# Top-32 attention with a squared-ReLU MLP: blocks of queries handled in pairs, PSUM banks fixed by purpose, MLP chunks of 512 rows

## Chip, cores and metric

One core of a Trainium2 chip. The metric is the device time of one execution in microseconds (us); lower is better.

## What is computed

```python
# q, k, v: (8, 8, 576, 64) float32; w_in: (512, 2048); w_out: (2048, 512)
scores = np.matmul(q, k.transpose(0, 1, 3, 2)) / np.sqrt(64)
kth    = np.partition(scores, -32, axis=-1)[..., -32:-31]      # the 32nd largest of a row
scores = np.where(scores >= kth, scores, -1e9)
attn   = softmax(scores)                                       # along a row
x      = matmul(attn, v) -> (8 * 576, 512)                     # heads side by side
out    = np.maximum(x @ w_in, 0) ** 2 @ w_out                  # (4608, 512) float32
```

## The kernel before

The program is written as a plan. Each operation is given an engine, an estimated duration, a priority (a due time), the tiles that it reads, writes and takes, and `schedule` turns the plan into one fixed order for each engine: when an engine is free, it takes the ready operation with the lowest priority. `Emitter` writes these orders out with semaphore waits. On the chip each engine then runs its own list in order and stands still at a wait.

**Blocks.** A row of scores has 576 columns. One block is 128 query rows of one head; the last 64 queries of both heads of a pair form one more block. 8 batches x 4 head pairs x 9 blocks are 288 blocks. `top_k` is called for a group of queries of a head pair and does its two blocks (three for the last group) with separate instructions for each block.

For one block (`top_k`, lines 443 to 573):

1. PE multiplies q and k in fp32 into two PSUM banks, 288 columns in each (`scores`, L365). One fp32 matmul appears in the trace as two passes; the two heads lie in different halves of the array's rows.
2. ACT copies the 576 scores to SBUF tile `s` (L464).
3. DVE takes the maximum of the two halves, one operand from PSUM: `m`, 288 wide (L528), then the maximum of the halves of `m`: `pp`, 144 wide (L535).
4. POOL makes the smaller values without comparing: it adds the two inputs as integers (L520, tiles `t1`, `t2`) and subtracts the maximum. The candidates lie in `f`: quarter maxima 0 to 144, their partners 144 to 288, the rest 288 to 576.
5. DVE finds eight values and strikes them out, three times (MAX8 and MATCH_REPLACE8): over 144, 144 and 288 columns. A last MAX8 over 576 columns (L561) gives the 32nd value, `kth`.
6. ACT makes `w` = relu(kth - s) in bf16, which is above zero where a score is to be dropped (L569).

`attend` then computes the scores once more, transposed (k times q, fp32, 64 rows of the array per head), adds `w` times a matrix with a very negative diagonal (`steep_bf`, the masks), and ACT takes the exponential out of PSUM (L628, L641). PE multiplies by v (`vb`, a column of ones gives the sum), DVE takes the reciprocal (L669), POOL scales (L671), PE transposes back. `feed` is the MLP over a chunk of rows: 576 rows of a batch in two halves of 288, the last batch as 320, 128 and 128.

The eight PSUM banks are one pool (`psum`); a tile of two banks or one bank goes wherever room is free. At the end `verdict` compares each kth with the eighth values struck out before. If one of the rounds had struck out too much, the whole program would be run again with full-width searches.

The constants `PER` (planned us per block), `T0` and `ME` (how much earlier than its block's other DVE work `m` is due) set the due times.

Of the kernel before, what the change touches and what calls it, by code (L numbers as in the profile page):

```python
# [12 lines left out]
P = 128  # L13
# [71 lines left out]
class Plan:  # L85
# [32 lines left out]
    def schedule(self, t0=0.0, latency=0.12, own=0.07):  # L118
# [162 lines left out]
def bass_top_k_attn__then__act_relu_squared_kernel(  # L281
# [11 lines left out]
    NHP = 4  # L293
# [8 lines left out]
    def sb(name, shape, dt=FP32, n=None):  # L302
# [3 lines left out]

    ident32 = sb("ident32", [P, P])
# [4 lines left out]
    kth = sb("kth", [P, 3, 4 * NPAIR + 8])  # L312
    c16 = sb("c16", [P, 3, 4 * NPAIR + 8])
    c24 = sb("c24", [P, 3, 4 * NPAIR + 8])
# [7 lines left out]

    sizes = {
        "rq": ([P, 5, 2, D], FP32, 2), "rk": ([P, 5, 2, D], FP32, 2), "rv": ([P, 9, D], FP32, 2),
        "qk": ([P, 2, S], FP32, 5), "vb": ([P, 10, D + 1], BF16, 5),
        "s": ([P, S], FP32, 8), "m": ([P, HALF], FP32, 4), "pp": ([P, QUART], FP32, 4),
        "t1": ([P, HALF], FP32, 2), "t2": ([P, QUART], FP32, 2), "f": ([P, S], FP32, 4),
        "a": ([P, 3, 8], FP32, 3), "sh": ([P, 3], FP32, 2), "w": ([P, S], BF16, 13),
        "p": ([P, 4, 2, 320], BF16, 3), "p4": ([P, 320], BF16, 3), "av": ([P, 5, D + 1], FP32, 2),
        "x": ([P, 5, D], BF16, 2), "xt": ([P, NCT, S], BF16, 3), "g": ([P, S], BF16, 16),  # L330
        "o": ([P, DM], FP32, 2), "ws": ([P, 1024], FP32, 2),
    }
    mem = {nm: sb(nm, *spec) for nm, spec in sizes.items()}
    pools = {nm: Pool(nm, spec[2]) for nm, spec in sizes.items()}
    ps32 = nc.alloc_psum_tensor("ps", [P, 8, 512], FP32)
    ps16 = ps32[:, :, :].bitcast(BF16)
    psum = Pool("psum", 8)
# [7 lines left out]
    def bank(t, i=0):  # L345
        return ps32[:, t.slot + i, :]
# [5 lines left out]

    def batch_order(b):
        if b < NB - 1:
            return ([(hp, g) for hp in range(NHP) for g in range(4)], {1: ([0, 1], False), 3: ([2, 3], True)},
                    [(0, S)])
        return ([(hp, g) for g in (2, 3, 0, 1) for hp in range(NHP)],
                {3: ([2, 3], True), 0: ([0], False), 1: ([1], False)}, [(256, 320), (0, 128), (128, 128)])

    PER = 3.2  # L360
    ME = 10
    T0 = 12.0
# [4 lines left out]
    def tr(o, i, ident):  # L367
# [557 lines left out]
```

## Time and profile before

| | |
|---|---|
| median of 3 runs | 1004.65 us (1004.55 to 1009.77) |
| profiled execution, its own time | 1005.76 us |
| span of its trace | 1003.8 us |
| mean granted TensorE clock | 0.968 |
| busy: PE, DVE, ACT, POOL | 910.8, 927.3, 765.0, 836.6 us |
| share of the span | 91%, 92%, 76%, 83% |

Busy time is the union of an engine's instructions. Instructions overlap at their ends (the next one starts while the last one drains), so the step from one start to the next is shorter than the mean duration of one; matmuls overlap most, and a busy PE is not PE at its peak.

### The profile page before, as it was taken

The numbers are of one execution on the slowest core, as the hardware profiler recorded it, in microseconds if no ns is written. First come the engines' busy times: TensorE is split into PE (matmuls) and PEld (weight loads), VectorE is DVE, ScalarE is ACT, GpSimd is POOL, SyncE is SP. The second block draws the span as 40 slices with busy tenths as digits, with TensorE's granted clock in tenths as the row PEclk, the third lists the DMA queues.
The fourth block names the chain that finished last, engine by engine and source line by source line (L and its number), as shares of the span: only waits on it lengthen the run. The fifth ranks groups of instructions, "written<-read, shape, count | busy, mean of one in ns | idle before, by whom it ended". The sixth has DMA issues, their size and how long they took to land.

```text
span 1003.8 us, 23634 instructions
## 1 busy us (share of the span) xinstructions
PE 910.8 (91%) x8082; PEld 537.9 (54%) x8082; DVE 927.3 (92%) x3538; ACT 765.0 (76%) x1341; POOL 836.6 (83%) x1391
## 2 busy tenths in 40 slices
PE   5677778999999999899999999899998999899996
PEld 3444444655555556555556555565565554456554
DVE  5999999999999999999999899999999999999920
ACT  4566668986799778897799868897788876668752
POOL 7998999888878888788888888797887878899941
PEclk9888799999999999999999999999999999899999
DMA  6643312011131102011211113101220110000001
GB/s 138 181 120 108 92 31 62 14 47 34 40 71 26 35 29 57 15 47 49 55 44 24 46 36 76 36 13 34 58 58 18 39 46 17 2 1 13 33 17 41
DMA packets 124417, 47.75 MB, mean 48 GB/s; under 512 B 116608, under 2 KB 116608, under 8 KB 124288
## 3 DMA queue, kind: packets, MB, share of 16 engines
q1 hardware_dynamic: 124288, 46.16, 18.1%
q8 instruction: 65, 1.06, 0.5%
q14 instruction: 64, 0.52, 0.2%
HBM read 36.70 MB, written 9.44 MB: 46 GB/s over the span
## 4 chain that ended last, share of the span: by engine, by line
POOL 36%; DVE 26%; PE 19%; issue 12%; ACT 5%; SPq 1%; DMA 1%; POOLq 0%; DVEq 0%
POOL f L520 18%; PE ps L365 18%; POOL t L520 13%; DVE kth L561 6%; DVE f L558 5%; DVE c L555 4%; DVE m L528 4%; DVE pp L535 3%; POOL x L671 2%; DVE f L549 2%; DVE a L547 2%; POOL vb L427 1%; ACT w L569 1%; ACT s L464 1%; ACT p L628 1%
## 5 line engine op out<-in xcount | busy, mean ns | idle before, releaser
L365 PE MATMUL ps<-qk 64*128 64x288 f32 (+7 forms) x2640 | 430.1, 438 | 45.3 <-DVE m L528 32.0
L365 PEld LDWEIGHTS ps<-qk 64*128 64x128 f32 (+1 forms) x2640 | 212.9, 181 | 169.8 <-DVE m L528 57.7
L569 ACT ACTIVATE w<-s,kth 128x576 bf16<-128x576 f32 x288 | 216.1, 776 | 28.4 <-DVE kth L561 27.4
L520 POOL TENSOR_TENSOR t<-s 128x288 int32<-128x288 int32 x288 | 229.2, 797 | 9.9 <-ACT s L464 7.5
L520 POOL TENSOR_TENSOR f<-t,m 128x288 int32<-128x288 int32 x288 | 223.9, 795 | 0.0
L464 ACT COPY s<-ps 128x576 f32<-128x576 f32 x288 | 170.8, 642 | 62.9 <-PE ps L365 62.3
L520 POOL TENSOR_TENSOR f<-t,pp 128x144 int32<-128x144 int32 x288 | 135.7, 489 | 99.4 <-DVE pp L535 99.2
L628 ACT ACTIVATE p<-ps 128x640 bf16<-128x640 f32 (+1 forms) x192 | 155.5, 812 | 74.2 <-PE ps L365 73.3
L558 DVE MATCH_REPLACE8 f<-c,f 128x144 f32<-128x144 f32 (+1 forms) x576 | 207.8, 368 | 0.0
L561 DVE MAX8 kth<-f 128x8 f32<-128x576 f32 x288 | 202.8, 747 | 0.0
L555 DVE MAX8 c<-f 128x8 f32<-128x144 f32 (+1 forms) x576 | 192.6, 372 | 2.1 <-POOL f L520 2.0
L365 PE MATMUL ps<-wo,g 128*128 128x512 bf16 (+1 forms) x640 | 158.8, 381 | 0.6 <-ACT xt L688 0.5
L365 PE MATMUL ps<-xt,win 128*128 128x288 bf16 (+2 forms) x1088 | 145.2, 283 | 5.4 <-DVE m L528 3.3
L528 DVE TENSOR_TENSOR m<-ps,s 128x288 f32<-128x288 f32 x288 | 126.8, 447 | 22.0 <-ACT s L464 18.2
L520 POOL TENSOR_TENSOR t<-m 128x144 int32<-128x144 int32 x288 | 141.4, 492 | 2.3
L365 PEld LDWEIGHTS ps<-steep_bf,w 128*128 128x128 bf16 (+1 forms) x1600 | 81.9, 101 | 108.5 <-issue 107.6
L365 PE MATMUL ps<-steep_bf,w 128*128 128x128 bf16 (+3 forms) x1600 | 121.9, 220 | 0.0
L535 DVE TENSOR_REDUCE pp<-m 128x144 f32<-128x288 f32 x288 | 116.1, 445 | 0.1
L365 PEld LDWEIGHTS ps<-xt,win 128*128 128x128 bf16 x1088 | 94.7, 99 | 37.6 <-DVE m L528 5.9
L365 PEld LDWEIGHTS ps<-wo,g 128*128 128x128 bf16 (+1 forms) x640 | 55.6, 100 | 57.3 <-issue 6.4
L549 DVE MATCH_REPLACE8 f<-a,pp 128x144 f32<-128x144 f32 x288 | 82.0, 293 | 0.0
L712 ACT ACTIVATE g<-ps 128x576 bf16<-128x576 f32 x112 | 71.9, 654 | 7.9 <-PE ps L365 6.8
(54 smaller groups left out, 780.8 us busy)
## 6 DMA issues: line engine op xcount, KB each, us to landing
rq<-in_q_dram SPq DMA_DIRECT2D x64, 128.0 KB, 2.4
rk<-in_k_dram SPq DMA_DIRECT2D x64, 128.0 KB, 2.5
rv<-in_v_dram SPq DMA_DIRECT2D x64, 128.0 KB, 2.4
out_dram<-o SPq DMA_DIRECT2D x32, 256.0 KB, 2.1
ws<-in_moe_w_in_dram SPq DMA_DIRECT2D x8, 512.0 KB, 5.2
ws<-in_moe_w_out_dram SPq DMA_DIRECT2D x8, 512.0 KB, 4.2
rq<-in_q_dram SPq DMA_DIRECT2D x32, 32.0 KB, 2.5
rk<-in_k_dram SPq DMA_DIRECT2D x32, 32.0 KB, 2.5
```

The lines of the kernel that those rows point to most:

```text
L365: return pe.matmul(o, l, r, start=start, stop=stop, skip_group_check=True)
L464: cp.append(pl.op("act", .64, tg - 28 + i, lambda i=i: act.copy(at(st[i])[:, :].rearrange("p (a c) -> p a c", a=2), ps32[:, ss[i].slot:ss[ ...
L520: return pl.op("gp", dur, prio + .8 * i, lambda: gp.tensor_tensor(o().bitcast(I32), x().bitcast(I32), y().bitcast(I32), op), **kw)
L528: dve(.43, lambda i=i: vec.tensor_tensor(at(m[i])[:, :], bank(ss[i])[:, 0:HALF], at(st[i])[:, HALF:S], ALU.max), dp=-ME, r=[ss[i]], hold=[ ...
L535: dve(.375, lambda i=i: vec.tensor_reduce(at(pp[i])[:, :], at(m[i])[:, :].rearrange("p (a c) -> p c a", a=2), AX.X, ALU.max), r=[m[i]], w= ...
L549: prev[i] = [dve(.275, lambda i=i: vec.match_replace(at(f[i])[:, 0:QUART], at(a)[:, i, :], at(pp[i])[:, :], NEG), r=[pp[i]], hold=[a], w=[ ...
L555: lambda i=i, t=t, wd=wd: vec.max(eighth(t, i), at(f[i])[:, 0:wd]),
L558: prev[i] = [chain(t, i, prev[i], dur + .06, lambda i=i, t=t, wd=wd: vec.match_replace(at(f[i])[:, 0:wd], eighth(t, i), at(f[i])[:, 0:wd], ...
L561: ks.append(chain(kth, i, prev[i] + [low[i]], .665, lambda i=i: vec.max(eighth(kth, i), at(f[i])[:, :]), hold=[f[i]]))
L569: pl.op("act", .75, tw + .8 * i, lambda i=i: act.activation(at(ws[i])[:, :], at(st[i])[:, :], ACTF.Relu, bias=kth[:, i, ix[i]:ix[i] + 1], ...
L628: return act.activation(o, i, ACTF.Exp, scale=0.125)
L712: return act.activation(at(g)[:, 0:nt].rearrange("p (a c) -> p a c", a=2), ps32[:, hh.slot:hh.slot + 2, 0:hw], ACTF.Relu)
```

## The change

- Two blocks are one unit. Their scores lie side by side in 1152 contiguous PSUM columns (three banks): five matmul pieces instead of four of 288 columns, the last one behind a wait on PE itself. One ACT copy of 1152, one `m` of 2x288, one reduction of 2x144 (written straight into `f`), and four POOL operations for the pair.
- The last 64 queries of two neighbouring head pairs form a unit of their own (`Z`). There are 144 units; `PER` becomes 6.0 for one unit.
- The three searches cover columns 0 to 104, 20 to 144 and 0 to 272 (before 0 to 144, 0 to 144, 0 to 288). The eighth value of the first is checked too (`c8`).
- `attend` no longer multiplies k by q: PE transposes `s` with the fp32 identity (nine 128x128 transposes for a pair), adds nine masks, and one ACT exponential reads 1152 columns.
- PSUM: banks 0 to 2 for scores, 3 to 5 for the transposed scores, one tile each; banks 6 and 7 for everything else.
- The MLP takes chunks of 512 rows; the 64-row remainders of six batches form one chunk of 384 rows, those of the last two lie in another.
- Weights are staged in the memory of `g`. The first loads of q, k and v wait for POOL to clear parts of `rv`.

```diff
-                        lat = own if v.eng == x.eng else latency
+                        lat = (own if x.eng != "pe" else .25) if v.eng == x.eng else latency
-    psum = Pool("psum", 8)
+    ps_s, ps_e, psum = Pool("ps_s", 1), Pool("ps_e", 1), Pool("psum", 2)
+    BASE = {"ps_s": 0, "ps_e": 3, "psum": 6}
...
+            PIECES = [[(0, 0, 0, 512, True), (1, 576, 512, 64, True), (1, 640, 0, 384, False), (1, 1024, 384, 128, True)],
+                      [(0, 512, 512, 64, False)]]
+            o_s = pl.op("pe", 1.2, tg - LEAD, lambda: fs(0), r=qu, w=[ss], take=[ss, st])
+            pl.op("pe", .15, tg - LEAD, lambda: fs(1), r=qu, w=[ss], after=[o_s])
+            cp = pl.op("act", 1.15, tg - LEAD + 1, lambda: act.copy(
+                at(st)[:, :, :].rearrange("p i c -> p (i c)"), wide(ss)), r=[ss], w=[st])
...
+                dve(.7, lambda: vec.tensor_tensor(
+                    at(m)[:, :, :], wide(ss).rearrange("p (i c) -> p i c", i=2)[:, :, 0:HALF],
+                    at(st)[:, :, HALF:S], ALU.max), dp=-ME, r=[ss], hold=[st], after=[cp], w=[m], take=[m])
+                big = dve(.67, lambda: vec.tensor_reduce(
+                    at(f)[:, :, 0:QUART], at(m)[:, :, :].rearrange("p i (a c) -> p i c a", a=2), AX.X, ALU.max),
+                    dp=-MQ, r=[m], w=[f], take=[f])
+                mid = whole(.87, tg - MP, ALU.subtract, lambda: at(f)[:, :, QUART:HALF], lambda: at(t2)[:, :, :],
+                            lambda: at(f)[:, :, 0:QUART], r=[t2], hold=[f], after=[big])
...
-                for t, wd, dur, more in ((c16, QUART, .215, None), (c24, HALF, .365, mid)):
+                for t, c0, c1 in ((c8, 0, 104), (c16, 20, QUART), (c24, 0, 272)):
...
+                        prev[i] = [chain(t, i, prev[i] + [mid], dur + .06,
+                                         lambda i=i, t=t, c0=c0, c1=c1: vec.match_replace(
+                                             at(f)[:, i, c0:c1], eighth(t, i), at(f)[:, i, c0:c1], NEG), hold=[f])]
...
+                for o, c, start in outs:
+                    tr(o, sf[:, c:c + 128], ident32[:, :], start=start, stop=True)
+                for o, c, start in outs:
+                    ins = mm(o, wf[:, c:c + 128], minus[:, :], False)
...
+            pl.op("act", 1.15, tt + 1, lambda: act.activation(
+                at(pt)[:, :, :].rearrange("p k q -> p (k q)"), wide(e), ACTF.Exp, scale=0.125), r=[e], w=[pt])
...
+        if o.eng == "sp":
+            o.deps.update(zeros)
```

DVE in the middle of the program; here are the rows of one unit before (`m` of later blocks stands between the searches; `pp`, `a`, `c` and `kth` are the steps above).

```order
L555 MAX c<-f 128x8 x2
L558 MATCH_REPLACE f<-c,f 128x144 x2
L555 MAX c<-f 128x8
L528 TENSOR_TENSOR m<-ps,s 128x288
L555 MAX c<-f 128x8
L528 TENSOR_TENSOR m<-ps,s 128x288
L669 RECIPROCAL rzall<-av 128x4
L558 MATCH_REPLACE f<-c,f 128x288 x2
L561 MAX kth<-f 128x8 x2
L535 TENSOR_REDUCE pp<-m 128x144 x2
```

DVE after, at the same place, with buffer numbers and waits (`s_gp` is POOL, `s_act` ACT, `s_dve` DVE itself): the start of unit f1, with the reduction of the next unit and an `m` between its own steps.

```order
1227 L563 TENSOR_REDUCE f1<-m1 128x2x144
1228 L563 TENSOR_REDUCE f2<-m2 128x2x144
1229 L578 MAX c8<-f1 128x8 [waits s_dve]
1230 L578 MAX c8<-f1 128x8
1231 L558 TENSOR_TENSOR m0<-ps,s3 128x576 [waits s_act]
1232 L582 MATCH_REPLACE f1<-c8,f1 128x104 [waits s_gp,s_dve]
1233 L582 MATCH_REPLACE f1<-c8,f1 128x104 [waits s_dve]
1234 L578 MAX c16<-f1 128x8 [waits s_dve] x2
```

Behind it: `m` and the reduction are one row for a pair, and the first MATCH_REPLACE of a unit waits for POOL, where before the third search did.

PE in the middle of the program after the change: scores of one unit (`qk`), transposes (`ident,s`) and masks (`steep_bf,w`) of another, and the transposes of a loaded k.

```order
L408 MATMUL ps<-qk 128x512 [waits s_dve]
L408 MATMUL ps<-qk 128x64
L408 MATMUL ps<-qk 128x384
L408 MATMUL ps<-qk 128x128
L411 MATMUL ps<-ident,s 128x128 [waits s_act]
L411 MATMUL ps<-ident,s 128x128 x3
L408 MATMUL ps<-steep_bf,w 128x128 x4
L408 MATMUL ps<-qk 128x64 [waits s_pe]
L411 MATMUL ps<-ident,rk 128x128 [waits d_rk0,s_act]
```

Behind it: every unit's scores wait for DVE's `m` of the unit before, which reads the same three banks.

The DMA queue at the start of the program after the change (before, the loads of q came first and without a wait).

```order
L826 DMA g<-in_moe_w_in_dram 128x1024 x2
L427 DMA rq<-in_q_dram 128x4x64 [waits s_gp]
L427 DMA rq<-in_q_dram 128x4x64
L429 DMA rq<-in_q_dram 64x2x64
L427 DMA rk<-in_k_dram 128x4x64 x2
```

Two transfers of weights now go ahead of the first loads.

## Rows read from the trace of the kernel before

**Rows 1.** The page: busy us, share of the span, instructions.

```profile
PE 910.8 (91%) x8082; PEld 537.9 (54%) x8082; DVE 927.3 (92%) x3538; ACT 765.0 (76%) x1341; POOL 836.6 (83%) x1391
```

**Rows 2.** Stretches: length, busy us of PE, PEld, DVE, ACT, POOL; clock, DMA.

```profile
50.00:150.00 100.00, 77.00 (x682) 46.54 (x681) 93.68 (x363) 65.88 (x113) 92.11 (x148) 0.83 0.32 87
...
400.00:600.00 200.00, 190.93 (x1707) 110.91 (x1706) 195.92 (x753) 164.82 (x289) 167.58 (x281) 0.99 0.16 41
...
940.00:970.00 30.00, 29.61 (x285) 18.72 (x285) 18.49 (x65) 19.00 (x41) 22.25 (x36) 1.00 0.07 24
```

**Rows 3.** DVE in order of time: start, length, line, operation, count.

```profile
503.17 1.18 DVE L535 TENSOR_REDUCE pp<-m 128x144 f32<-128x288 f32 x3
504.27 0.72 DVE L547 MAX8 a<-pp 128x8 f32<-128x144 f32 x3
...
507.55 0.82 DVE L555 MAX8 c<-f 128x8 f32<-128x288 f32 x2
...
510.64 2.07 DVE L561 MAX8 kth<-f 128x8 f32<-128x576 f32 x3
```

**Rows 4.** Groups by shape, DVE and POOL: count, busy us, mean ns, idle before.

```profile
L528 DVE TENSOR_TENSOR m<-ps,s 128x288 f32<-128x288 f32 x288 | 126.8, 447 | 22.0 <-ACT s L464 18.2 <-POOL f L520 2.1
L561 DVE MAX8 kth<-f 128x8 f32<-128x576 f32 x288 | 202.8, 747 | 0.0
...
L555 DVE MAX8 c<-f 128x8 f32<-128x288 f32 x288 | 119.3, 448 | 2.0 <-POOL f L520 2.0
...
L520 POOL TENSOR_TENSOR t<-s 128x288 int32<-128x288 int32 x288 | 229.2, 797 | 9.9 <-ACT s L464 7.5
...
L520 POOL TENSOR_TENSOR f<-t,pp 128x144 int32<-128x144 int32 x288 | 135.7, 489 | 99.4 <-DVE pp L535 99.2
```

**Rows 5.** PE in order of time, 500 to 513 us, and a run at 938 us.

```profile
501.67 1.13 PE L365 MATMUL ps<-qk 64*128 64x256 f32 x8
502.74 0.62 PE L365 MATMUL ps<-steep_bf,w 128*128 128x128 bf16 x8
503.31 1.24 PE L365 MATMUL ps<-qk 64*128 64x288 f32 x8
...
504.97 0.66 PE L368 MATMUL ps<-ident,rq 128*128 128x128 f32 x4
...
938.17 1.89 PE L365 MATMUL ps<-wo,g 128*128 128x512 bf16 x8
```

**Rows 6.** PE groups on the page: count, busy us, mean ns.

```profile
L365 PE MATMUL ps<-qk 64*128 64x288 f32 (+7 forms) x2640 | 430.1, 438 | 45.3 <-DVE m L528 32.0
...
L365 PE MATMUL ps<-wo,g 128*128 128x512 bf16 (+1 forms) x640 | 158.8, 381 | 0.6 <-ACT xt L688 0.5
L365 PE MATMUL ps<-xt,win 128*128 128x288 bf16 (+2 forms) x1088 | 145.2, 283 | 5.4 <-DVE m L528 3.3
...
L365 PE MATMUL ps<-steep_bf,w 128*128 128x128 bf16 (+3 forms) x1600 | 121.9, 220 | 0.0
```

**Rows 7.** ACT groups by shape: count, busy us, mean ns.

```profile
L464 ACT COPY s<-ps 128x576 f32<-128x576 f32 x288 | 170.8, 642 | 62.9 <-PE ps L365 62.3
...
L628 ACT ACTIVATE p<-ps 128x640 bf16<-128x640 f32 x128 | 90.0, 707 | 35.5 <-PE ps L365 34.9
...
L628 ACT ACTIVATE p<-ps 128x1024 bf16<-128x1024 f32 x64 | 65.4, 1022 | 38.7 <-PE ps L365 38.4
```

**Rows 8.** The first microseconds in order of time, and the weight loads on the page.

```profile
11.21 0.46 DVE L528 TENSOR_TENSOR m<-ps,s 128x288 f32<-128x288 f32 x1 [11.21 <-ACT s L464]
...
ws<-in_moe_w_in_dram SPq DMA_DIRECT2D x8, 512.0 KB, 5.2
```

**Rows 9.** The end: the last kth, ACT's last copy; a PE group from 940 to 970.

```profile
954.10 1.41 DVE L561 MAX8 kth<-f 128x8 f32<-128x576 f32 x2
...
996.08 0.59 ACT L745 COPY o<-ps 128x512 f32<-128x512 f32 x1 [3.08 <-PE ps L365]
...
L365 PE MATMUL ps<-xt,win 128*128 128x320 bf16 x64 | 10.1, 300 | 0.0
```

More of the change, by code (lines that the diff above doesn't have):

```diff
@@ L305, in sb @@
         return [nc.alloc_sbuf_tensor(f"{name}{i}", shape, dt) for i in range(n)]
+    PER = 6.0
+    T0 = 12.0
+    LEAD = 20
+    ME = 10
+    MQ = 0
+    MP = 3
+    LAG = 20
+    STEP = 3.2
     ident32 = sb("ident32", [P, P])
@@ L560, in top_k @@
-                for i in range(nb):
-                    ks.append(chain(kth, i, prev[i] + [low[i]], .665, lambda i=i: vec.max(
-                        eighth(kth, i), at(f[i])[:, :]), hold=[f[i]]))
+                dve(.7, lambda: vec.tensor_tensor(
+                    at(m)[:, :, :], wide(ss).rearrange("p (i c) -> p i c", i=2)[:, :, 0:HALF],
+                    at(st)[:, :, HALF:S], ALU.max), dp=-ME, r=[ss], hold=[st], after=[cp], w=[m], take=[m])
+                whole(1.45, tg, ALU.add, lambda: at(t1)[:, :, :], lambda: at(st)[:, :, 0:HALF],
+                      lambda: at(st)[:, :, HALF:S], r=[st], w=[t1], take=[t1])
@@ L578, in top_k @@
+                return st, wt
+            for i in range(2):
+                o = pl.op("gp", .75, tw + 1.3 * i, lambda i=i: gp.tensor_scalar(
+                    at(f)[:, i, :], at(st)[:, i, :], kth[:, i, n:n + 1], STEEP, ALU.subtract, ALU.mult),
+                    r=[st], hold=[f], after=[ks[i]])
                 pl.op("gp", .75, tw + 1.3 * i + .65, lambda i=i: gp.tensor_scalar(
-                    at(ws[i])[:, :], at(st[i])[:, :], BIG, at(sh)[:, i:i + 1], ALU.min, ALU.max),
-                    r=[st[i], sh], w=[ws[i]], take=[ws[i]])
@@ L685, in fx, with out_x @@
                 return ins
             pl.op("pe", .05 * nu + .1, tt + 5, fx, r=[xr], w=[xp], take=[xp])
-            pl.op("act", .19 + nq / 1200, tt + 6, lambda: act.copy(
-                at(xt)[:, hp, col:col + nq], ps16[:, xp.slot, 0:nq]), r=[xp], w=[xt], take=[xt] if first_xt else [])
-        def feed(b, tok, nt, xt, tm, step, end):
-            last = b == NB - 1
+            xt, col, first = parts
+            def out_x():
+                nq = 64 * nu
+                if gi != Z:
+                    return act.copy(at(xt)[:, hp, col:col + nq], half(xp)[:, 0:nq])
+                return act.copy(at(xt)[:, hp:hp + 2, col:col + 64],
+                                half(xp)[:, 0:128].rearrange("p (i q) -> p i q", i=2))
@@ L694, in feed @@
+            pl.op("act", .19 + nu / 20, tt + 6, out_x, r=[xp], w=[xt], take=[xt] if first else [])
+        def feed(chunk, xt, tm, step):
+            nt = sum(n_ for _, _, n_ in chunk)
+            b = chunk[-1][0]
+            last, end = b == NB - 1, chunk is CHUNKS[-1]
             kf = max(1, 512 // nt)
-            nh = 2 if nt > 512 else 1
-            hw = nt // nh
+            lag = 0 if last else LAG
             gs = [tile("g") for _ in range(NFB // kf)]
             for i, g in enumerate(gs):
-                hh = Tile(psum, nh)
+                hh = Tile(psum)
@@ L771, in build @@
[L771 to L777 removed]
+                hps = (hp, hp if gi != Z else hp + 1)
```

475 lines of the change are left out of this document (213 added, 262 removed).

## Prediction

> **What bounds the kernel now.** I read the page first, then stretches of the span, then each engine's list in order of time. On the page DVE (927.3 us) and PE (910.8) are both above 90% [rows 1], so their shares alone do not tell which sets the pace. The stretches do. From 400 to 600 us DVE is busy 195.92 of 200 us, while PE shows 190.93, ACT 164.82 and POOL 167.58 [rows 2]; PE's figure contains the draining ends of its matmuls. DVE's own idle time is small: all 288 `m` together wait 22.0 us, and the 288-wide searches wait 2.0 us for POOL [rows 4]. So DVE, with its fixed list, is the bound in the body. At the end it is PE: the last kth is ready at 955.5 (954.10 + 1.41), yet the last output copy starts at 996.08 [rows 9], and from 940 to 970 PE is busy 29.61 of 30 us [rows 2].
>
> The span of 1003.8 thus divides into 11.2 us before DVE's first instruction [rows 8], 944.3 us to the last kth, and 48.3 us behind it. The profiled execution took 1005.76 us; the median of the runs is 1.1 us below that.
>
> **DVE, the main term.** I take steps from start to start, since neighbours overlap. Two MAX8 of 288 take 0.82 where one lasts 0.448: a step of 0.37. Three of 144 take 0.72 and three of 576 take 2.07, which gives steps of about 0.21 and 0.66 [rows 3, 4]. A step is thus about 0.06 us plus 1.04 ns for each column. For `m` and the reduction I take 0.365 for 288 inputs (three reductions take 1.18 [rows 3]), hence 0.665 for one of 576.
> - Pairing `m` and the reduction saves a fixed part each: 2 x (0.73 - 0.665) = 0.13 us per pair.
> - The searches lose 40, 20 and 16 columns; each is a MAX8 and a MATCH_REPLACE8 in two blocks: 76 x 4 x 1.04 ns = 0.32 us per pair. The 576-wide last search stays.
> - 0.45 us x 144 pairs = **64 us less**. Some 17 reciprocals more cost about 1.5 us.
>
> DVE's list then lasts about 865 us, 5.9 us per pair.
>
> Whether a removed instruction gives back its whole duration or only its fixed step is decided here. By the rows an instruction starts 0.08 us before the one ahead of it ends [rows 3, 4], so only the step counts. The Trainium skill, "VectorE: DVE Perf Modes", section "The DRAIN you can't avoid", says that the next operation does not start until the pipeline is empty. The trace does not agree: the overlap is in the rows, so I keep the step. What whole durations would give is among the rivals.
>
> **A new wait on that path.** The first MATCH_REPLACE8 of a pair now waits for POOL's subtraction, because it overwrites what POOL reads. That subtraction can start only behind the reduction and lasts about 0.8 us (a 288-element operation takes 797 ns [rows 4]). Between the reduction and the waiting instruction the order puts two short MAX8 (0.34 us) and mostly an `m` or the next reduction (0.66 each), so 1.0 to 1.7 us. With semaphores the work fits in most places. Nothing to all is between 0 and about 0.5 us x 144 = 72 us; since the cover is there in the order, I take +5 us for this and for waits at `m` together.
>
> **POOL and ACT.** A POOL element costs (797 - 489) / 144 = 2.1 ns, so an operation on 576 takes about 1.41 us and a pair costs 2 x (1.41 + 0.80) = 4.4 instead of 5.2 us: some 105 us less in all, with squares for a few more chunks (+15) on top. ACT's one copy of 1152 and one exponential of 1152 cost about 1.1 us each by the slope between 640 and 1024 columns ((1022 - 707) / 384 = 0.82 ns [rows 7]), slightly less than now. Neither sets the pace, so I count nothing; the fifth DMA of each v load is on a queue with room.
>
> **PE, the resource that gets tighter.** Steady steps: eight fp32 passes of 288 take 1.24 us with the last one's 0.44 in it; eight masks 0.62; four fp32 transposes 0.66; eight matmuls of 512 take 1.89 with 0.38 in it, 0.215 each or 0.42 ns per bf16 column [rows 5, 6].
> - Scores: today the two heads alternate, and one pass of each head streams beside one of the other, so four matmuls cost about 1.0 us per pair. Now one head has one 512-column matmul, the other three in a row, and the remaining 64 columns come alone. Counting what cannot lie side by side, 512 + 512 + 384 + 128 + 128 + 128 columns at the 0.84 ns of today's passes: about 1.5 us. **+0.5 us per pair.**
> - Transposed scores: 2.0 us per pair now (for four blocks 2 x (1.07 + 0.57) from the starts in [rows 5], and 0.8, four passes and four masks, for the last 64 keys); nine transposes at about 0.13 and nine masks at about 0.07: 1.8 us. **-0.2 us.**
> - MLP: the first product keeps its columns, the second has 36 row blocks instead of 40, since the half-filled ones of 64 rows go: 64 matmuls x 0.215, about **-15 us in all**.
>
> By steps, PE's work is now about 2640 x 0.12 + 640 x 0.215 + 1088 x 0.12 + 1600 x 0.058 [rows 6] plus some 95 us for v, loads and transposes: 775 us. It becomes about 775 + 43 - 15 = 800 us. In a span of 945 that is 85%, against 77% now. It fits, but waits cost more.
>
> **Start.** Two 512 KB weight loads (5.2 us to landing [rows 8]) now go ahead of q, and q waits for POOL's clearing. That is 2 to 5 us; the first unit needs 1.5 times the score work and a copy twice as long, 1 to 2 us more. DVE starts at 14 to 18 us. I take **+5**.
>
> **End.** Behind the last kth of the new order PE has about 61 matmuls of 512, 112 of 128 columns and one unit's transposes and products: 13 + 6.5 + 2.5 = 22 us, plus two relus of 576 before (1.3, as copies of that width [rows 7]) and what follows ACT's last copy today (7.7). That is 32 to 37 us against 48.3, if PE is on schedule; being tighter, it may bring a backlog along. Between 0 and -15 I take **-8**.
>
> **Sum.** 1005.8 - 64 + 1.5 + 5 + 5 - 8 = 945 us, so far from 1004.65 that the 1.1 us do not matter.
>
> **The rivals.**
> - *Everything fits better* (start hidden, PE on time, end -15): 1005.8 - 64 + 1.5 + 3 - 15 = about 930 down to 918. For it: POOL and ACT both get freer. Against: two single PSUM buffers and a third of two banks, each a ring. 0.10.
> - *Whole durations count.* Then pairing gives 2 x (2 x 0.447 - 0.747) = 0.29 us per pair instead of 0.13, so 88 instead of 64 us: 921. Against: by this count DVE's 288-wide groups alone could not fit their busy time (288 x 0.448 = 129 us against 119.3 [rows 4]). It is the rule of the section named above. 0.03.
> - *PE becomes the bound.* From 940 to 970 PE set the pace [rows 2]; its 285 instructions there (64 of them 320 columns wide [rows 9]) come to about 26 us by the steps above, so it can use about 88% of the time. 800 / 0.88 = 909, plus about 60 for the start and the first hundred us, in which there is little MLP work (77.00 busy of 100 from 50 to 150): about 970. For it: PE already shows 95% busy in the body. Against: that figure is inflated. 0.22.
> - *One buffer for scores* (slower). Scores, copy and `m` now form a ring: 1.5 + 1.1 + 0.7 us and three semaphores, about 3.6 us of a 5.9 us period. But each of the three stands in an in-order list; if PE, ACT and DVE together hold it up by over 2.3 us, DVE stands still at `m`. At 0.5 us per pair on top of the sum the time is 945 + 72 = 1017; the change turns into a loss from about 0.45 us per pair. For it: `m` and `s` already waited with eight banks (22.0 and 62.9 us [rows 4, 7]). Against: `m` is ordered some 5 us apart. 0.07.
> - *The clock falls with the transposes.* From 50 to 150 us the granted clock is 0.83 [rows 2], so both levels (1.2 and 2.4 GHz) occur in this kernel. If it averaged 0.9 throughout, PE would need 800 / 0.9 / 0.88 + 40 = 1050 us. Against: the run of four fp32 transposes [rows 5] lies in a stretch with 0.99 [rows 2]. 0.03.
> - *The change doesn't do what it says.* Narrower first searches could trip the check and run everything a second time, about 1900 us. In the reference's own draw the smallest distance between an eighth value and kth is 0.0007 over all 36864 rows, on the safe side: 0.01. Or short instructions cost a fixed minimum and only the pairing pays: 1005.8 - 19 + 4 = 990: 0.03.
>
> **Chances.** Forecast 0.51 (own range 932 to 958). The range from 918 to 985 takes in the better fit, the whole durations and most of the PE-bound case. 0.5% is 5 us, about what a measurement of this kernel can tell. Faster: 0.51 + 0.10 + 0.03 + 0.22 + 0.03 less a little for the upper tail = 0.87; same 0.03; slower 0.10.
>
> **What would show it.** Right: DVE busy near 865 us and over 96% in the body; reduction and `m` near 0.75 us each; MAX8 of 104 and 124 with durations near 0.26 and 0.28; DVE's first instruction at 14 to 18 us; 33 to 45 us behind the last kth. Wrong: idle time before `m` in the tens of us with ACT's copy as its releaser (ring); waits of MATCH_REPLACE8 on POOL; DVE below 93% with PE full (PE-bound); a granted clock below 0.95.

## The result, and the profile after

The changed kernel takes **968.74 us** (median of 4 runs, 963.22 to 972.14) against 1005.14 us for the kernel before beside it: a ratio of 0.9623, 95% interval 0.9569 to 0.9677. That is faster, inside the range of 918 to 985 and 24 us above the forecast of 945. The profiled execution took 972.14 us, the longest of the four, so the sum is held against that: 27 us too low. Ratios compare runs in the undisturbed (fast) state alone; other runs occurred in experiment 4 only, whose median over all six lies above what its ratio gives.

The page after, engines and the chain that ended last (columns as in [rows 1]):

```profile
PE 887.8 (91%) x7650; PEld 620.2 (64%) x7650; DVE 863.3 (89%) x3269; ACT 737.5 (76%) x1133; POOL 750.4 (77%) x794
...
PE 44%; DVE 30%; POOL 10%; ACT 8%; issue 6%; DMA 0%; SPq 0%; POOLq 0%; DVEq 0%
```

DVE's busy time fell from 927.3 [rows 1] to 863.3 us, by 64.0; the sum had 64 less and 1.5 more for reciprocals, so 62.5. The single operations came out as costed too. Groups by shape, DVE after (columns as in [rows 4]):

```profile
L558 DVE TENSOR_TENSOR m<-ps,s 128x576 f32<-128x576 f32 x144 | 107.9, 749 | 45.2 <-ACT s L504 41.9 <-POOL f L555 2.8
L563 DVE TENSOR_REDUCE f<-m 128x288 f32<-128x576 f32 x144 | 106.4, 752 | 0.2
...
L578 DVE MAX8 c<-f 128x8 f32<-128x124 f32 x288 | 73.4, 282 | 0.0
L582 DVE MATCH_VALUE_LOAD f<-c,f 128x8 f32 x864 | 70.9, 82 | 9.6 <-POOL f L555 9.5
...
L578 DVE MAX8 c<-f 128x8 f32<-128x104 f32 x288 | 61.8, 257 | 0.2
```

What the sum missed is DVE's idle time. Stretches from DVE's first instruction to the end of the last kth (length, DVE busy, clock, DMA share, GB/s), first of the kernel before, then after:

```profile
11.21:50.00 38.79, 36.73 (x138) 0.90 0.69 169
50.00:150.00 100.00, 93.68 (x363) 0.83 0.32 87
150.00:820.00 670.00, 661.16 (x2532) 0.99 0.17 41
820.00:955.50 135.50, 129.60 (x491) 0.97 0.04 14
```

```profile
15.86:50.00 34.14, 25.60 (x91) 1.00 0.59 142
50.00:150.00 100.00, 85.91 (x328) 0.81 0.31 89
150.00:800.00 650.00, 639.94 (x2434) 1.00 0.17 43
800.00:935.14 135.14, 106.62 (x404) 1.00 0.06 19
```

Length minus busy time is idle time: before 2.1 + 6.3 + 8.8 + 5.9 = 23 us, after 8.5 + 14.1 + 10.1 + 28.5 = 61 us. In the body hardly anything was lost (DVE is busy 98.5% of 650 us); 37 of the 38 us more lie in the first 150 and the last 135 us. What DVE waited for, of the changed kernel (total, times, longest; first from 16 to 152 us, with what PE waited for there, then from 800 to 935 us):

```profile
DVE m L558 <- ACT s L504: 35.5, 10, 15.9
PE ps L408 <- DVE m L558: 14.0, 11, 2.3
PE ps L411 <- ACT w L593: 5.9, 3, 2.8
```

```profile
DVE rzall L654 <- ACT av L652: 11.8, 7, 2.8
DVE f L582 <- POOL f L555: 8.3, 9, 2.6
DVE m L558 <- ACT s L504: 3.4, 4, 1.5
DVE kth L585 <- POOL f L555: 2.4, 1, 2.4
DVE m L558 <- POOL f L555: 2.2, 1, 2.2
```

The 15.9 us of the first row is the time before DVE's first instruction, so 19.6 us of waits at `m` are left in the first batch. In the last batch it is other waits: reciprocals wait for the products with v (11.8 us), and the strikes, `m` and one kth wait for POOL (12.9 us).

It helps to cut the span at two rows, the first kth of the second batch and that of the last one (DVE in order of time, before and after):

```profile
140.73 1.40 DVE L561 MAX8 kth<-f 128x8 f32<-128x576 f32 x2
...
839.16 1.42 DVE L561 MAX8 kth<-f 128x8 f32<-128x576 f32 x2
```

```profile
15.86 0.76 DVE L558 TENSOR_TENSOR m<-ps,s 128x576 f32<-128x576 f32 x1 [15.86 <-ACT s L504]
...
22.25 0.76 DVE L558 TENSOR_TENSOR m<-ps,s 128x576 f32<-128x576 f32 x1 [4.36 <-ACT s L504]
...
151.98 1.42 DVE L585 MAX8 kth<-f 128x8 f32<-128x576 f32 x2
...
803.31 1.41 DVE L585 MAX8 kth<-f 128x8 f32<-128x576 f32 x2
...
933.72 1.42 DVE L585 MAX8 kth<-f 128x8 f32<-128x576 f32 x2 [2.38 <-POOL f L555]
```

| us | first batch with the start | six middle batches | last batch with the end |
|---|---|---|---|
| before | 140.7 | 698.4 | 164.6 |
| after | 152.0 | 651.3 | 167.0 |
| change | +11.3 | -47.1 | +2.4 |
| the sum, cut the same way | -2.2 | -43.1 | -15.2 |

The last row spreads DVE's 62.5 us and the 5 us of waits evenly over eight batches and puts the start's +5 and the end's -8 where they belong. The middle came out as predicted, a little better. The first part missed by 13.5 us and the last by 17.6. Part of the first miss is this one execution: in other executions of the same first lists that part took 144.8 to 152.6 us (experiment 7). Behind the last kth the gain is more than expected (35.2 us instead of 48.3), but the last batch ahead of it took 132 us to its last kth instead of 116, and more than gave it back.

### The profile page after: what moved, and what is told of

Its sections match the earlier page's. It is cut to its first block, busy times and chain, and to the rows that moved or that the text cites. A ratio compares the mean times of both kernels' runs of the same rounds, so it can differ in the third digit from the quotient of the medians.

```text
span 970.3 us, 21522 instructions
## 1 busy us (share of the span) xinstructions
PE 887.8 (91%) x7650; PEld 620.2 (64%) x7650; DVE 863.3 (89%) x3269; ACT 737.5 (76%) x1133; POOL 750.4 (77%) x794
## 4 chain that ended last, share of the span: by engine, by line
PE 44%; DVE 30%; POOL 10%; ACT 8%; issue 6%; DMA 0%; SPq 0%; POOLq 0%; DVEq 0%
PE ps L408 34%; PE ps L411 10%; DVE f L582 8%; DVE c L578 7%; DVE kth L585 6%; POOL f L555 6%; DVE m L558 5%; POOL t L555 3%; DVE f L563 3%; ACT p L626 3%; ACT s L504 2%; ACT w L593 1%; ACT g L706 1%; POOL x L656 1%; DMA rk<-in_k_dram 0%
## 5 line engine op out<-in xcount | busy, mean ns | idle before, releaser
L408 PE MATMUL ps<-qk 64*128 64x512 f32 (+6 forms) x1600 | 281.7, 413 | 30.0 <-DVE m L558 28.3
L582 DVE MATCH_REPLACE8 f<-c,f 128x104 f32<-128x104 f32 (+2 forms) x864 | 268.7, 320 | 0.0
L578 DVE MAX8 c<-f 128x8 f32<-128x104 f32 (+2 forms) x864 | 248.5, 325 | 0.2
L555 POOL TENSOR_TENSOR t<-s 128x576 int32<-128x576 int32 x144 | 201.6, 1411 | 25.2 <-ACT s L504 25.1
L411 PE MATMUL ps<-ident,s 128*128 128x128 f32 x1296 | 204.1, 286 | 6.8 <-ACT w L593 6.3
L504 ACT COPY s<-ps 128x1152 f32<-128x1152 f32 x144 | 161.4, 1121 | 64.1 <-PE ps L408 62.8
L555 POOL TENSOR_TENSOR f<-t,m 128x576 int32<-128x576 int32 x144 | 202.8, 1408 | 0.0
L626 ACT ACTIVATE p<-ps 128x1152 bf16<-128x1152 f32 x144 | 162.9, 1131 | 35.1 <-PE ps L408 34.3
L411 PEld LDWEIGHTS ps<-ident,s 128*128 128x128 f32 x1296 | 146.4, 144 | 35.5 <-ACT w L593 8.5
L558 DVE TENSOR_TENSOR m<-ps,s 128x576 f32<-128x576 f32 x144 | 107.9, 749 | 45.2 <-ACT s L504 41.9
L408 PE MATMUL ps<-wo,g 128*128 128x512 bf16 x576 | 143.4, 380 | 1.0 <-ACT xt L681 0.4
L656 POOL TENSOR_TENSOR x<-av,rzall 128x256 bf16<-128x256 f32 (+1 forms) x88 | 47.1, 535 | 58.6 <-DVE rzall L654 58.2
```

The costliest lines, as they stand in the source:

```text
L408: return pe.matmul(o, l, r, start=start, stop=stop, skip_group_check=True)
L411: return pe.matmul(o, i, ident, is_transpose=True, skip_group_check=True, **kw)
L504: cp = pl.op("act", 1.15, tg - LEAD + 1, lambda: act.copy(at(st)[:, :, :].rearrange("p i c -> p (i c)"), wide(ss)), r=[ss], w=[st])
L555: return pl.op("gp", dur, prio, lambda: gp.tensor_tensor(o().bitcast(I32), x().bitcast(I32), y().bitcast(I32), op), **kw)
L558: dve(.7, lambda: vec.tensor_tensor(at(m)[:, :, :], wide(ss).rearrange("p (i c) -> p i c", i=2)[:, :, 0:HALF], at(st)[:, :, HALF:S], ALU.m ...
L578: lambda i=i, t=t, c0=c0, c1=c1: vec.max(eighth(t, i), at(f)[:, i, c0:c1]),
```

## The experiments

Each kernel was timed in five rounds beside the kernel before. "First, middle, last" are the three parts of the table above in each kernel's profiled execution.

**1. The loads of q, k and v first again.**

```diff
+    for o in main.ops[:n_pre]:
+        if o.eng == "sp":
+            o.deps.update(zeros)
```

> Edit: the weights' loads, too, wait for POOL's clearing of the v buffers, so the first q, k and v loads are issued ahead of them, as in the kernel before. Theory A (the start counts through: DVE's first instruction came at 15.9 us instead of 11.2, and all later work hangs behind it): DVE's first instruction 3 to 4 us earlier, at about 12 us, the first kth 3 to 4 us earlier, and the time 3 to 8 us less than the changed kernel's 968.7 us, so 961 to 966. Rival B (what PE has to do in the last 135 us, where it was 99% busy and DVE idle for up to half, decides the end, and a head start of DVE is only waited away there): first instruction earlier, but DVE's idle time after 800 us grows by the same 3 to 4 us and the time stays at 968 +/- 2 us.

Measured: 969.25 us, ratio 0.9626 (0.9593 to 0.9659): no gain. First, middle, last 146.8, 656.1, 167.5. DVE started earlier, but the span is the same 970.3 us:

```profile
13.51 0.76 DVE L558 TENSOR_TENSOR m<-ps,s 128x576 f32<-128x576 f32 x1 [13.51 <-ACT s L504]
...
931.17 1.40 DVE L585 MAX8 kth<-f 128x8 f32<-128x576 f32 x2
```

The time is the one that rival B named, but not by its working. The first kth of the second batch came 5.2 us earlier, that of the last batch only 0.4: the lead was lost in the middle, which took 4.8 us longer, and not in the last batch, whose DVE idle time did not grow (26.2 instead of 28.5 us). The lists of PE, ACT and DVE differ from those of the changed kernel from about 146 us on; why the middle took longer stays open. A lead is not lost always: in experiment 7 it came through.

**2. The wide searches again.**

```diff
-                for t, c0, c1 in ((c8, 0, 104), (c16, 20, QUART), (c24, 0, 272)):
+                for t, c0, c1 in ((c8, 0, QUART), (c16, 0, QUART), (c24, 0, HALF)):
```

> Edit: the first three searches of a pair of blocks run over 144, 144 and 288 columns again, as before the change, instead of 104, 124 and 272. DVE gets 76 x 4 columns x 1.04 ns = 0.32 us per pair back, 46 us in 144 pairs. Theory A (DVE sets the pace from about 150 to 800 us, PE only in the last 135 us): the body's 650 us grow by 5.5% or 35 us, the ends hardly: 968.7 + 30 to 42 = about 1000 to 1010 us, and DVE's busy time near 909 us. Rival B (PE or the ring through the single scores buffer sets the pace nearly everywhere, and DVE's shorter list brought little): at most + 15 us, so below 984 us, with DVE over 93% busy.

Measured: 999.79 us, ratio 0.9927 (0.9901 to 0.9954). First, middle, last 150.3, 684.8, 160.4: the middle grew by 33.4 us, and 6 batches x 18 pairs x 0.32 = 34.6. From 400 to 600 us DVE has nothing left to wait for (all engines; columns as in [rows 2]):

```profile
400.00:600.00 200.00, 184.70 (x1631) 129.68 (x1651) 199.27 (x725) 165.37 (x253) 152.62 (x155) 1.00 0.17 42
```

Theory A: DVE's list sets the pace of the body, and only there. The last part became 6.6 us shorter although its DVE work grew.

**3. The last batch but one split.**

```diff
-        if b == 0:
+        if b in (0, NB - 2):
...
-    CHUNKS.append([(NB - 2, 0, 512)])
+    CHUNKS += [[(NB - 2, 0, 256)], [(NB - 2, 256, 256)]]
```

> Edit: the last batch but one is worked like the first: its query blocks 0 and 1 for all pairs of heads, then 2 and 3, then the short ones, and its MLP in two chunks of 256 rows instead of one of 512, so the first half of it can run while that batch is still worked on. About 64 matmuls of 512 columns for the first product and 32 for the second (96 x 0.215 = 20 us of PE work, less what the shorter chunks' lag leaves) move from the last batch (where PE was 99.5% busy and the batch took 131 us instead of 109) to the batch before it (where DVE was the bound and PE had some 5% left). Theory A (PE bound in the last 135 us because of MLP work that collects there): DVE's last kth 8 to 14 us earlier, the time 8 to 14 us less, 955 to 961 us. Rival B (PE is as full in the batch before: what moves there lengthens it by as much): DVE's idle time moves from after 800 us to before it, and the time stays at 968 +/- 3 us. Rival C (it is the order of the last batch itself, not the work brought along): same time, last batch still over 125 us.

Measured: 970.99 us, ratio 0.9631 (0.9602 to 0.9659): no gain. First, middle, last 149.1, 651.8, 168.6. The last batch took 140.0 us, so rival C fits in both its signs. Why is not shown; one guess, that the batch which was to take the work was already full with the 384-row chunk, led to experiment 8.

**4. The short piece of the scores first.**

```diff
+            PIECES = [[(0, 512, 512, 64, True)], [(0, 0, 0, 512, True)],
+                      [(1, 576, 512, 64, False), (1, 640, 0, 384, False), (1, 1024, 384, 128, True)]]
...
+            o_s = pl.op("pe", .15, tg - LEAD, lambda: fs(0), r=qu, w=[ss], take=[ss, st])
+            o_m = pl.op("pe", .45, tg - LEAD, lambda: fs(1), r=qu, w=[ss], order=[o_s])
+            pl.op("pe", .75, tg - LEAD, lambda: fs(2), r=qu, w=[ss], after=[o_s], order=[o_m])
```

> Edit: of one pair's scores the 64 columns that stand alone behind everything else, with a wait on PE's own counter, come first; the 512 columns of the same head follow without a wait, then the other head's three matmuls, which alone wait for the 64 (they share a PSUM bank with them). The same columns are computed. In the trace of the changed kernel the lone piece costs about 0.36 us of PE per pair from its start to the next instruction, and lies in the ring scores, copy, pair maximum. Theory A (PE and the ring are what is late): PE's work falls by 0.15 to 0.3 us per pair, the last 135 us become shorter by 3 to 6 us and the waits for the copy in the first 150 us by some us: 955 to 965 us. Rival B (PE's own time for the scores is the same in whatever order, since the waiting moves between the pieces): same time, 968 +/- 3 us, with the same 1.8 us per pair in PE's steps.

Measured: 1123.75 us, ratio 1.1031 (1.0991 to 1.107): far slower than both kernels, which neither theory expected. First, middle, last 176.7, 758.8, 184.9. One unit's scores on PE in order of time, in the changed kernel and in this one (the granted clock is 1.00 in both stretches; rows without `qk` are other work):

```profile
504.44 1.36 PE L408 MATMUL ps<-qk 64*128 64x512 f32 x8 [0.60 <-DVE m L558]
505.74 0.81 PE L408 MATMUL ps<-vb,p 128*128 128x65 bf16 x20
506.47 0.43 PE L408 MATMUL ps<-qk 64*128 64x64 f32 x2
506.83 0.66 PE L411 MATMUL ps<-ident,s 128*128 128x128 f32 x4
```

```profile
551.54 0.43 PE L408 MATMUL ps<-qk 64*128 64x64 f32 x2
551.91 1.04 PE L408 MATMUL ps<-wo,g 128*128 128x512 bf16 x4
552.88 1.12 PE L408 MATMUL ps<-qk 64*128 64x512 f32 x2
553.93 0.81 PE L408 MATMUL ps<-vb,p 128*128 128x65 bf16 x20
554.66 1.35 PE L408 MATMUL ps<-qk 64*128 64x64 f32 x6
555.95 0.66 PE L411 MATMUL ps<-ident,s 128*128 128x128 f32 x4
```

In the changed kernel eight passes of both heads take 1.30 us to the next instruction, since the 512 columns of one head run beside the other head's three pieces. Here the planner put other products between the heads. By the starts the 512 columns alone take 1.05 us and the other head's three pieces 1.29, and with the short piece a pair costs PE 2.7 us instead of 1.7. Summed over the execution in this way, the scores took 402 us of PE instead of 263, its lower clock included; the span grew by 150. From the first piece to the end of the last a unit took 4.5 us here instead of 2.5. DVE waited at `m` much longer, 157.2 us in all instead of 41.9 (16 of either before its first instruction), but PE hardly waited for DVE. From 400 to 500 us, all engines; then DVE's wait in the whole execution and PE's for `m` from 400 to 500 us:

```profile
400.00:500.00 100.00, 98.07 (x752) 62.88 (x763) 90.60 (x339) 78.56 (x119) 71.28 (x73) 1.00 0.16 39
```

```profile
DVE m L559 <- ACT s L505: 157.2, 110, 16.0
...
PE ps L408 <- DVE m L559: 0.2, 1, 0.2
```

If the ring through the single scores buffer set the pace, PE would stand still at `m` as well. It did so for 0.2 of 100 us. So at full clock this experiment shows PE as the bound, made so by 1 us more per pair, and says nothing on the ring. What the low clock added is not separated: the granted clock of this execution was 0.927 instead of 0.976, and 0.64 from 50 to 150 us.

**5. Half of the late second product left out, old order.**

```diff
-                        for fb in range(4 * sub, 4 * sub + 4):
+                        for fb in range(4 * sub, 4 * sub + (2 if b >= NB - 2 else 4)):
```

> Edit: the order of all instructions stays that of the changed kernel, but the second MLP product of the chunks of the last two batches (9 blocks of rows) leaves out 2 of each 4 matmuls, so half of the sum over the 16 blocks of the hidden layer is missing there: 72 matmuls of 512 columns, 72 x 0.216 us = 15.6 us of PE work less, all of it after about 800 us. Theory A (the last 135 us are set by PE's own throughput): the time falls by nearly all of it, 11 to 16 us, to about 953 to 958 us, and DVE's idle time after 800 us falls by about 10 us. Rival B (there it is waits on the fixed order of the lists, and PE's busy share is only draining ends): less than 5 us, above 963 us.

Measured: 964.08 us, ratio 0.9572 (0.9546 to 0.9597): 4.7 us less (the interval overlaps the changed kernel's, 0.9569 to 0.9677, but lies below that of experiment 6). First, middle, last 147.2, 653.1, 162.5. The last batch and the end, all engines, in the changed kernel and here:

```profile
800.00:935.10 135.10, 133.05 (x1063) 85.30 (x1061) 106.58 (x404) 101.80 (x169) 107.89 (x117) 1.00 0.06 19
935.10:970.30 35.20, 25.44 (x233) 16.49 (x230) 5.22 (x17) 10.65 (x22) 4.30 (x6) 0.92 0.14 41
```

```profile
800.00:931.30 131.30, 122.49 (x1006) 79.58 (x1003) 103.61 (x391) 98.76 (x164) 104.89 (x114) 1.00 0.06 19
931.30:962.80 31.50, 19.31 (x197) 12.84 (x197) 5.17 (x16) 10.47 (x22) 4.31 (x6) 0.86 0.16 45
```

PE was busy 98.5% of the last batch, and with less work it merely stood idle there (8.8 us instead of 2.1). Rival B: within fixed lists the saving is lost to waits. The Trainium skill, "Perfetto Trace Analysis", section "Identifying the Most-Contended Engine", says that TensorE's busy share is no good measure of how near it is to its limit. The trace agrees that the share alone misleads: 98.5% did not mean that 15.6 us less work would save 15.6 us. Experiment 11 shows that the reason here is the lists.

**6. The same in the body** (`b in (2, 3)` in the place of `b >= NB - 2`).

> Edit: the same omission, but in the second MLP product of the chunks of batches 2 and 3 (8 blocks of rows, worked between about 380 and 590 us): 64 matmuls, 13.8 us of PE work less, in the stretch in which DVE is idle by less than 1 us per 50. Theory A (DVE sets the pace there, PE has room): no gain, 968 +/- 3 us; the batches from 370 to 584 us still take about 107 us each. Rival B (PE is the bound throughout): 8 to 14 us less, like the late omission.

Measured: 968.16 us, ratio 0.9619 (0.9601 to 0.9637): no gain. First, middle, last 152.6, 650.8, 167.4. Theory A: PE has room in the body, as far as the old lists can show it.

**7. Useless transposes at the start.**

```diff
+            more = 1 * (not full and state["n"] <= 14)
...
-                for o, c, start in outs:
+                for o, c, start in outs * (1 + more):
                     tr(o, sf[:, c:c + 128], ident32[:, :], start=start, stop=True)
```

> Edit: in the first 14 pairs of blocks (to about 100 us) each fp32 transpose of the scores is done twice into the same place, 14 x 9 = 126 transposes more, 126 x 0.109 = 14 us of useless PE work where PE is busy only 36 of 50 us, has no MLP work yet, and its granted clock is 0.70 (50 to 100 us). Theory A (the slow start is the clock: at its lower level the ring scores, copy, pair maximum takes longer than a pair's 6 us and DVE idles 22.6 us in the first 150 us): the granted clock of 50 to 150 us rises from 0.81 to over 0.95, DVE's idle time in the first 150 us falls by 8 us or more, and the time falls by 5 to 12 us. Rival B (the clock does not depend on this work, or the ring's wait is the order of the lists and not the clock): clock as before or waits as before, the time 968 to 978 us, up by some of the 14 us.

Measured: 962.85 us, ratio 0.9573 (0.9545 to 0.96): 5 to 6 us less with 126 transposes more (6 by the medians, 5 by the ratios; the interval lies below that of experiment 6). First, middle, last 142.6, 651.8, 167.3: only the first part changed. From 50 to 150 us, DVE:

```profile
50.00:150.00 100.00, 96.17 (x364) 0.97 0.37 99
```

The granted clock rose from 0.81 to 0.97, and DVE is busy 96.17 us instead of 85.91. The planner was told of the longer transposes, so the first lists differ a little as well. Kernels whose first 150 us are the same program speak without that: in the changed kernel and experiments 5, 6, 9, 10 and 11 the clock of this stretch happened to be 0.81, 0.90, 0.83, 0.90, 0.90 and 0.83, and DVE was busy 85.9, 91.8, 86.9, 91.8, 94.3 and 87.8 us. Their first parts took 151.4 to 152.6 us at 0.81 to 0.83 and 144.8 to 149.0 at 0.90; with 0.97 here and 0.98 in experiment 12 it was 142 us. So the clock is the cause of most of what the first part lost. At the lower level (1.2 GHz) the eight passes took 2.4 us from their start to the next instruction instead of 1.3; in the changed kernel, in a stretch with a granted clock of 0.50:

```profile
89.24 2.51 PE L408 MATMUL ps<-qk 64*128 64x512 f32 x8
93.14 0.69 PE L408 MATMUL ps<-qk 64*128 64x64 f32 x2
```

There the ring of scores, copy and `m` took 4.6 + 1.1 + 0.7 = 6.4 us, more than DVE's 6.0 us of work for a pair (863.3 / 144); at full clock it takes 2.5 + 1.1 + 0.7 = 4.3. The lower clock is not all: even at 0.97 DVE idled 13.3 us in the first batch, against 8.4 in the kernel before at 0.83.

The Trainium skill, "TensorE: Matmul & The Clock Gate", Part 4, says that transposes do not count as activity for the clock as matmuls do. This trace does not agree: transposes were all that was added, and the clock rose to 0.97 (0.98 in experiment 12, which has them too), where no other kernel here went over 0.92 in that stretch.

**8. Late PE work spread, and PE's costs corrected.**

```diff
+    ZB = 4
-    CHUNKS.append([(b, 512, 64) for b in range(NB - 2)])
-    CHUNKS.append([(NB - 2, 0, 512)])
+    CHUNKS.append([(b, 512, 64) for b in range(ZB)])
+    CHUNKS.append([(b, 512, 64) for b in range(ZB, NB - 2)])
+    CHUNKS += [[(NB - 2, 0, 256)], [(NB - 2, 256, 256)]]
...
-                    pl.op("pe", 1.0, to + lag + step * sub, fo,
+                    pl.op("pe", .88, to + lag + step * sub, fo,
```

> Edit: the same computation in another order. The rows 512 to 575 of batches 0 to 5, one chunk of 384 rows that the MLP works on in batch 6, become two chunks, of batches 0 to 3 (256 rows, worked on in batch 4) and 4 and 5 (128 rows); the last batch but one is worked like the first, with its MLP in two chunks of 256; and the planner's costs of PE's operations are set to the steps read from the trace of the changed kernel (scores 1.15 + 0.32 instead of 1.2 + 0.15 us, four and five transposes with their masks 0.68 and 0.84 instead of 0.75 and 0.95, four matmuls of 512 columns 0.88 instead of 1.0, and so on), which changes the order of all lists. The experiment that only split the last batch but one did not help; theory A says why: the batch to which its work moved was already full with the 384-row chunk. Then this one, which empties that batch too, takes 10 to 22 us off, to about 947 to 959 us, with the last batch under 128 us instead of 131 and the batch before it under 111. Rival B (the last batch is slow by its own order, whatever MLP work is left for it): 968 +/- 4 us.

Measured: 966.76 us, ratio 0.9607 (0.9593 to 0.9621). First, middle, last 144.9, 665.5, 152.2: the last part fell by 14.8 us, and the middle rose by 14.2. Theory A missed: the last batch still took 129.1 us and the one before it 111.7, and the time is the one that rival B named. What fell is the end behind the last kth, 23.1 us instead of 35.2. So late work could be moved away from the end, but as much time came back in the body. Whether that is the moved work or the lists made with lower costs was not separated.

**9 and 10. POOL's late squares on one column, alone and with the omission of 5.**

```diff
+                    c_ = w_ if b < NB - 2 else 1
-                        at(g)[:, 0:w_], at(g)[:, 0:w_], at(g)[:, 0:w_], ALU.mult), u=[g])
+                        at(g)[:, 0:c_], at(g)[:, 0:c_], at(g)[:, 0:c_], ALU.mult), u=[g])
```

> Edit: the order of all instructions stays that of the changed kernel, but POOL's 36 squares of the MLP chunks of the last two batches (33.6 us between 800 and 940, 20 of 512 columns at 1.04 us and 16 of 384 at 0.82) take the first column of their tile alone, so the other columns go into the second product unsquared; some 30 us of POOL work less there. The late omission of PE work shortened the last batch by only 1 us, so PE's throughput alone is not what holds it up. Theory A (POOL is late in the last batch: it was busy 45.9 of 50 us from 850 to 900, DVE waited there for POOL's subtractions 8.3 + 2.4 + 2.2 us, and POOL's reciprocal products wait behind its own squares): the last batch takes 112 to 122 us instead of 131 and the last kth comes 9 to 19 us earlier; the end behind it may grow, the time 4 to 15 us less. Rival B (the fixed order of the lists is enough to hold DVE up, POOL's load does not matter): last batch still over 127 us, time 965 to 969 us. Rival C (PE and POOL are both at their limit there and each covers for the other): about as little as for PE, 1 to 4 us, and much more when both are relieved.

> Edit: both late omissions at once, in the same order of instructions: POOL's 36 squares of the last two batches on one column, and 72 of the 144 matmuls of their second product left out (15.6 us of PE work). Theory A (POOL holds the last batch up): as with POOL relieved alone, plus the 4 us at the end that PE's omission gave: the time 8 to 19 us under 968.7. Rival B (order of the lists): as with PE's omission alone, about 964 us. Rival C (both at their limit, each covering for the other): last batch under 115 us and the time below 952 us, more than the two single gains together.

Measured: 968.61 us, ratio 0.9606 (0.9585 to 0.9627), for POOL alone, last part 167.2: nothing. With both 961.59 us, ratio 0.954 (0.9517 to 0.9563), last part 159.3, its batch still 129 us to the last kth. Within the old lists POOL's load is not what holds the batch up. Of the two together 2.5 us more comes through than of PE alone, which the intervals do not separate, and far less than rival C wants. POOL relieved with lists made anew was not tried, so its part in them stays open.

**11. The omission of 5, with new lists.**

```diff
-                    pl.op("pe", 1.0, to + lag + step * sub, fo,
+                    pl.op("pe", 1.0 if b < NB - 2 else .5, to + lag + step * sub, fo,
```

> Edit: the late omission of PE work again (72 of the 144 matmuls of the last two batches' second product, 15.6 us), but now the planner is told of it (those pieces cost it 0.5 us instead of 1.0), so the lists of all engines are made anew for the smaller work. Theory A (the last 170 us are PE's: the planner, to which PE is full there, gives up DVE's time to keep PE going, so what PE has to do decides the time, but through the order of the lists, and a saving inside an old order is lost to its waits): the time falls by 10 to 14 us, to 955 to 959 us, most of it behind the last kth, while the last batch stays over 130 us. Rival B (no order helps, the last batch is slow whatever PE has to do): 963 to 966 us, as with the omission in the old order.

Measured: 957.73 us, ratio 0.9503 (0.9476 to 0.9529): 11 us less, where the old order gave 4.7. First, middle, last 151.4, 651.3, 158.0; the last batch took 135.8 us and the end behind it 22.3. This is theory A in time and in place: what PE has to do decides the last part, by way of the order.

**12. A version that beats both.**

```diff
-    LEAD = 20
+    LEAD = 24
-    LAG = 20
+    LAG = 14
...
-                    tm = T0 + PER * state["n"] + (20 if not last else 8)
+                    tm = T0 + PER * state["n"] + (20 if not last else 0)
```

with `ZB` from 8 and `more` from 7.

> Edit, on the whole computation: the useless second transposes in the first 14 pairs, which kept PE's clock up, and an order with the late PE work spread: the rows 512 to 575 of batches 0 to 5 in two chunks (batches 0 to 3, and 4 and 5) instead of one, scores issued 24 instead of 20 us ahead, the lag of the MLP 14 instead of 20 us and that of the last batch's MLP 0 instead of 8. The planner's costs stay as they were. Theory A (start lost to the clock, end lost to PE work that collects): 6 us from the start as in the run with the second transposes alone and 4 to 8 us from the end: 955 to 959 us, faster than both kernels. Rival B (the earlier reordering brought only 2 us, so spreading does not help): 959 to 964 us.

Measured: **954.78 us** (954.38 to 956.83), ratio 0.9493 (0.9471 to 0.9515), below the changed kernel's whole interval. First, middle, last 142.1, 654.1, 158.6: 9.8 and 8.5 us gained, 2.8 given back. Which of the changed constants did how much was not separated. Stretches of DVE:

```profile
15.84:50.00 34.16, 24.16 (x86) 0.95 0.63 147
50.00:150.00 100.00, 97.22 (x368) 0.98 0.35 98
150.00:800.00 650.00, 636.95 (x2419) 0.99 0.17 42
800.00:918.66 118.66, 100.72 (x382) 1.00 0.05 17
```

## Why the prediction was right, and where it was off

- **DVE's 64 us**: right within 1.5 us in busy time, and term by term. From start to start `m` and the reduction give 16.9 us less (18.7 predicted), the searches 48.3 (46), the reciprocals 1.5 more (1.5). The middle batches gave 47.1 us where the sum had 43.1. Steps, not whole durations, were the right measure: by whole durations 88 us would have gone. The Trainium skill, "VectorE: DVE Perf Modes", section "The DRAIN you can't avoid", says that the next operation waits for the pipeline to empty, and in the same paragraph that one that is not held starts earlier. The prediction cited the first alone; the rows, with 0.08 us of overlap, fit the second.
- **The start, +5**: DVE's first instruction came 4.7 us later. That part held.
- **"I take +5 us for this and for waits at `m` together"** is the first step that failed. POOL's new wait cost 9.5 us, 8.3 of them in the last batch, and DVE's idle time between its first instruction and the last kth grew by 38 us. In the first batch it is the waits at `m`, 19.6 of 22.6 us: in its stretches at the lower clock the ring of the single scores buffer takes longer than DVE's work for a pair, as experiment 7 shows. The kernel before had a clock of 0.83 from 50 to 150 us and lost only 6.3 us in that stretch, with eight banks to run ahead in. The prediction looked at this clock only as a rival for the whole span and did not price it for the stretch in which it is low anyway.
- **"It fits" and the end's -8** is the second. PE's 800 us were set against the whole span (85%), as if they lay evenly. They don't: in the first 153 us there is no MLP work at all, and of what the change saves behind the last kth a part moved ahead of it. In columns, the MLP matmuls of the last batch grew from 94,208 to 150,528 and those behind the last kth fell from 71,680 to 48,128. MLP groups on PE from 800 to 935 us:

```profile
L408 PE MATMUL ps<-wo,g 128*128 128x512 bf16 x148 | 36.5, 380 | 0.2 <-ACT av L652 0.2
L408 PE MATMUL ps<-xt,win 128*128 128x512 bf16 x108 | 26.8, 380 | 0.0
L408 PE MATMUL ps<-xt,win 128*128 128x384 bf16 x64 | 12.2, 327 | 0.7 <-ACT g L706 0.6
```

  At steps of 0.216 us for 512 columns and 0.163 for 384 that is 256 x 0.216 + 64 x 0.163 = 66 us in 135, half of the time; from 400 to 510 us the same groups count 132 of 512 columns, 28.5 us in 110, a quarter. DVE idled 28.5 us there, and still 26.0 to 28.2 when work was taken from PE or POOL inside the old lists; with lists made anew for 15.6 us less of PE work the time fell by 11 us. That the planner, to which PE is full there, spaces DVE's work accordingly is the likely reading; no run shows the planner's own times.
- **The rivals.** "PE becomes the bound" named 970 us and is nearest to the result, but not by its own working: it had PE as the bound throughout, and experiments 2 and 6 show DVE as the bound for 650 us. It holds for the last part alone. The single buffer cost the 19.6 us of waits at `m` in the first batch and 6.4 us behind it, so it did not turn the change into a loss. The prediction's 22.0 us of waits at `m` before the change hold 11.2 us ahead of DVE's first instruction, so with eight banks such waits were only half as long as it took them to be. The clock did not fall with the transposes (1.00 from 150 us on). "Whole durations" and "everything fits" are out.
- **PE's small terms**: the scores of a pair take 1.30 + 0.36 us by the starts above; 1.5 had been predicted.
- **Open**: what lengthened the middle of experiments 1 and 8, how much of the first 150 us is the clock and how much the order of the lists, and what POOL's waits in the last batch would cost with other lists.

## What to carry to other kernels

Cut the span into stretches before pricing a change: the same saving was worth all of its 8 us per batch in the middle and nothing at the two ends, where another resource was late. With lists that are fixed ahead, work taken from an engine pays far more if the lists are made anew (11 against 4.7 us for the same 15.6). Where one PSUM buffer replaces many, price its ring at the lowest clock that the trace shows. And when an experiment makes a kernel slower, look at which engine has no idle time left before calling a longer wait elsewhere the cause.

## What was not expected of the hardware

- Useless work bought time: 126 fp32 transposes more, some 14 us of PE, raised the granted clock of 50 to 150 us from 0.81 to 0.97 and made the kernel 5 to 6 us faster.
- The same program gets a different clock from run to run: the four runs of the changed kernel had mean clocks of 0.976, 0.977, 0.986 and 0.979 and took 972.14, 969.23, 963.22 and 968.25 us. Experiment 12, with 0.987 to 0.993, spread over 2.5 us only.
- Scores of two heads in different halves of the array's rows run beside each other almost for nothing: at a clock of 1.00 the 512 columns of one head alone take 1.05 us, the other head's three pieces alone 1.29, both together 1.30. The order that parted them cost PE 1.0 us more per pair.
